# Weight magnitudes, float64 exponents and the leaky activation on ScalarE, c21 read from PSUM, and turn steps on either of two engines

## The chip, the core and the metric

The kernel runs on one core of one Trainium2 chip. The core has a matrix engine (PE; its weight loads are listed as PEld), a vector engine (DVE), a scalar engine (ACT), a general engine (POOL) and a sync engine (SP) that issues the DMAs. Each engine works through its own instructions strictly in program order; a semaphore holds an instruction, and all behind it, until what it needs is done. The metric is the device time of one execution in microseconds.

## The reference

Three layers follow one another. All arithmetic is float32, apart from the last layer's weights, which arrive as float64.

```python
# retention: B=4, H=8, S=576, D=64
scores = scale * np.matmul(q, k.transpose(0, 1, 3, 2))
ret = scores * Dmat[None, :, :, :]
x = np.matmul(ret, v)                 # -> (2304, 512)
# mixture: 8 experts, F=1024
P = np.exp(logits - logits.max())     # logits = x @ w_gate
for _ in range(8):
    P /= P.sum(1, keepdims=True) + 1e-09
    P /= P.sum(0, keepdims=True) + 1e-09
    P *= N / E
out += P[:, e:e + 1] * (np.maximum(x @ w1[e], 0.0) @ w2[e])
# feed-forward: d_ff=2048, float64 weights
h = x @ w_in
g = np.maximum(0.01 * h, h)
return g @ w_out
```

## The kernel before

**Units and stages.** The retention fills about the first 106 us. After it the two other layers are cut into 20 units of 512 hidden columns: units 0 to 15 are the mixture (two units per expert), units 16 to 19 the feed-forward layer. A unit runs through three stages of 384 token pairs, a stage through two groups g. Every group has seven *h products* (`product_h`, matmuls of line L916: inputs times first weights), and every stage 3 x 7 *second products* (`group_s`, L1089: hidden values times second weights). These are Strassen-like schemes with seven products in place of eight, so operands are sums and differences of quarter blocks. Units 0 and 15 (`PLAIN`) use an ordinary second product (L1131). Each float32 operand is split into a high and a low float16 part, and three of the four partial products are taken.

**Between the products.** ACT and DVE empty the banks. In a group the h products come in the order 1, 5, 6, 2, 7, 3, 4. Products 1, 6, 7 and 4 build on one another through ACT copies from bank to bank: hA to hB (L926), hB to hD (L943). c11, c12 and c22 end up in `fp`, c21 (from bank hD, L961) in the fourth quarter of `fs`, a buffer of which there is one. `splits` then queues the high parts (ACT, L999), the low parts (DVE, L1009 and L1006) and the sums and differences that the second products need (d1 L988, d2 L1037, d3 L1039, d4 L988 or L990). d1 and d3 read c21. In the feed-forward layer each block is first made leaky on DVE (L982). The second products are added into `y` by DVE (L1102); an ACT copy (L1107) seeds one bank from another.

**Weights.** While a unit runs, the next unit's weights are prepared (`prep_steps`): eight reductions on DVE find the largest magnitude of 512 columns each (`amax`, L167), L173 folds them, a matmul with ones (L179) adds the maxima of all partitions into every partition, and DVE turns the sum into a power of two (`pow2`, `recip2`). ACT scales the raw weights (L195), ACT makes the high parts (L210, L239), POOL the low parts and the block sums (L220, L227, L245). `idle_bank` lends such small matmuls the one of the two banks s1a and s1b that the pair of second products under way does not use; the next pair starts in that bank.

**Float64.** In units 0 to 14 the float64 weights come in 64 pieces: DVE masks mantissa and exponent (L343, L344), shifts the exponent's bias and clamps it (`first2`, L350 and L351), ACT makes the mantissa (L358), DVE joins the parts (L367, L368), POOL multiplies (L375).

**The turn.** Behind unit 15 (`turn_steps`) each block of `y` is normed by the sum of its magnitudes (ACT, L1207), scaled on POOL (L1223), transposed on PE, copied from the bank by ACT (L1235), and cut into operands: POOL sums, high parts on ACT (L477), low parts on DVE (L480), a store to DRAM and a load back (`x<-x`) for units 16 to 19.

**What sets the order.** No loop on the chip: the program is straight, and its order is worked out while it is written. PE's order is fixed in the main (`seconds_by`). `Order` keeps a clock of its own and a booked end for each engine (`COST`); at every tick it takes from its queues the tasks whose inputs are done by its booking and whose engine is free within 0.6 us (`SLACK`). `flush` forces what must stand before a product. `lat` is the extra time that a task is to stand behind its inputs.

## Time and profile before

| | us |
|---|---|
| median of three runs | 1950.81 (1947.8 to 1951.41) |
| the profiled execution | 1949.6 |
| its span, first to last instruction | 1947.8 |
| busy: PE / DVE / ACT / POOL | 1802.0 / 1697.6 / 1135.9 / 839.2 |
| mean granted clock of PE | 0.977 of full |

The span and the execution's own time lie 1.8 us apart. Stretches are given in us from the span's start; u3 is unit 3. In a row of the trace, busy time is the union of the instructions' times, while the mean is of one instruction: PE's matmuls overlap, so a mean of 330 ns does not mean that each costs 330 ns. "Idle before" is the time that the engine stood still just before such instructions, and the releaser is what ended it.

### The profile page before, as it was taken

To read this page: it belongs to the slowest core of one execution; us is meant where nothing else is said; L and a number is where in the kernel's file an instruction comes from. 1 tells how busy PE (TensorE), PEld (TensorE's weight loads), DVE (VectorE), ACT (ScalarE), POOL (GpSimd) and SP (SyncE) were. 2 spreads that over 40 slices of the span, in tenths; PEclk is the share of its full clock that TensorE was granted. 3 is DMA by queue.
4 is the path that set the end of the run, shared out by engine and by line. 5 is a ranking of instruction groups with operands and counts; after the bars stand their busy time and mean duration, and the time that the engine had idled before them with its cause. 6 is when DMAs were issued, how large, how long until landed. Compare 5 with 4: busy or idle time off the path is not lost.

```text
span 1947.8 us, 35674 instructions
## 1 busy us (share of the span) xinstructions
PE 1802.0 (93%) x13699; PEld 1298.0 (67%) x13699; DVE 1697.6 (87%) x2877; ACT 1135.9 (58%) x2294; POOL 839.2 (43%) x786
## 2 busy tenths in 40 slices
PE   8879999899999989999999999999999967899997
PEld 7744477677677767776776777677775545566776
DVE  6756799999999999999999999999866757699986
ACT  5645656465656656565665656465556557556542
POOL 4725353443627253452536254352428625273400
PEclk8889999999999999999999999999999989899999
DMA  8863353444454453444444354345343532343242
GB/s 309 300 215 116 127 179 115 144 130 141 133 163 123 127 180 107 147 136 155 125 151 146 111 179 130 123 133 179 97 126 109 191 122 78 119 139 97 76 126 76
DMA packets 207855, 276.64 MB, mean 142 GB/s; under 512 B 13874, under 2 KB 177860, under 8 KB 202564
## 3 DMA queue, kind: packets, MB, share of 16 engines
q1 hardware_dynamic: 207684, 274.37, 44.8%
q8 instruction: 107, 1.75, 0.4%
q14 instruction: 64, 0.52, 0.1%
HBM read 244.69 MB, written 29.63 MB: 141 GB/s over the span
## 4 chain that ended last, share of the span: by engine, by line
DVE 47%; PE 39%; issue 4%; POOL 4%; DMA 3%; ACT 2%; SPq 0%; DVEq 0%; ACTq 0%; POOLq 0%
DVE y L1102 10%; PE s L1089 6%; DVE hs L1009 6%; PE hB L916 5%; PE hA L916 5%; PE s1a L1089 5%; PE hE L916 5%; PE s1b L1089 4%; DVE fs L988 4%; DVE hp L1006 3%; DVE hp L1009 3%; PE hD L916 2%; DVE fs L1039 2%; DVE fs L1037 2%; PE s L1131 2%
## 5 line engine op out<-in xcount | busy, mean ns | idle before, releaser
L916 PEld LDWEIGHTS <-w 128*128 128x128 f16 x5040 | 495.5, 99 | 304.2 <-issue 34.8
L1089 PEld LDWEIGHTS <-hs 128*128 128x128 f16 x3888 | 381.3, 98 | 118.8 <-DVE hs L1009 19.2
L1089 PEld LDWEIGHTS <-hp 128*128 128x128 f16 x2916 | 287.0, 98 | 126.6 <-issue 50.4
L220 POOL TENSOR_TENSOR w<-raw,w 128x384 f16<-128x384 f32 x152 | 173.3, 1156 | 354.2 <-ACT w L210 354.2
L227 POOL TENSOR_TENSOR raw<-raw 128x256 f32<-128x256 f32 x304 | 289.6, 953 | 19.6
L916 PE MATMUL hE<-x,w 128*128 128x384 f16 x1440 | 278.4, 330 | 16.1 <-DMA x<-x 7.4
L916 PE MATMUL hB<-x,w 128*128 128x384 f16 x1440 | 276.6, 328 | 11.8 <-ACT hB L926 9.3
L916 PE MATMUL hA<-x,w 128*128 128x384 f16 x1440 | 278.8, 330 | 8.5 <-POOL w L220 7.1
L1089 PE MATMUL s<-w,hs 128*128 128x256 f16 x1944 | 266.3, 273 | 6.8 <-ACT s L1107 6.4
L999 ACT ACTIVATE hs<-fs 128x768 f16<-128x768 f32 (+1 forms) x228 | 188.0, 825 | 136.3 <-DVE fs L988 72.2
L245 POOL TENSOR_TENSOR w<-raw,w 128x512 f16<-128x512 f32 x148 | 201.4, 1376 | 119.1 <-ACT w L239 119.0
L1009 DVE TENSOR_TENSOR hs<-fs,hs 128x768 f16<-128x768 f32 (+1 forms) x228 | 238.1, 1057 | 5.5 <-ACT hs L999 5.4
L1102 DVE SCALAR_TENSOR_TENSOR y<-s,fac,y 128x256 f32<-128x256 f32 (+1 forms) x324 | 196.5, 608 | 52.3 <-PE s L1089 34.9
L375 POOL TENSOR_TENSOR f<-f,e 128x256 f32<-128x256 f32 x64 | 52.1, 813 | 394.7 <-DVE e L368 393.1
L999 ACT ACTIVATE hp<-fp 128x384 f16<-128x384 f32 x240 | 158.2, 678 | 39.9 <-DVE fp L954 27.6
L1089 PE MATMUL s1a<-w,hp 128*128 128x256 f16 x972 | 135.9, 277 | 28.6 <-DVE y L1102 28.6
L1089 PE MATMUL s1b<-w,hs 128*128 128x256 f16 x972 | 135.5, 273 | 13.6 <-DVE hs L1009 8.2
L1089 PE MATMUL s1a<-w,hs 128*128 128x256 f16 x972 | 137.6, 278 | 10.2 <-DVE hs L1009 5.9
L1089 PE MATMUL s1b<-w,hp 128*128 128x256 f16 x972 | 132.7, 273 | 12.1 <-DVE y L1102 11.9
L961 ACT ACTIVATE fs<-hD 128x384 f32<-128x384 f32 x120 | 58.8, 490 | 143.4 <-DVE hs L1009 96.7
L916 PE MATMUL hD<-x,w 128*128 128x384 f16 x720 | 137.9, 328 | 1.0 <-ACT hD L943 0.4
L1089 PE MATMUL s<-w,hp 128*128 128x256 f16 x972 | 133.9, 274 | 0.4 <-ACT s L1107 0.4
(175 smaller groups left out, 2773.1 us busy)
## 6 DMA issues: line engine op xcount, KB each, us to landing
x<-x SPq DMA_DIRECT2D x420, 384.0 KB, 4.1
raw<-in_wm SPq DMA_DIRECT2D x32, 1024.0 KB, 6.2
r<-in_wf SPq DMA_DIRECT2D x64, 256.0 KB, 3.3
qk<-in_qk SPq DMA_DIRECT2D x16, 512.0 KB, 6.8
vk<-in_vk SPq DMA_DIRECT2D x16, 512.0 KB, 4.8
wf_s<-f SPq DMA_DIRECT2D x32, 256.0 KB, 3.6
raw<-wf_s SPq DMA_DIRECT2D x8, 1024.0 KB, 5.2
x<-xst SPq DMA_DIRECT2D x30, 256.0 KB, 2.0
```

The lines of the kernel that those rows point to most:

```text
L220: nc.gpsimd.tensor_tensor(v[0], v[1], v[2], op=ALU.subtract)
L227: nc.gpsimd.tensor_tensor(o, x, y_, op=ALU.subtract)
L245: (nc.gpsimd if u or part else nc.vector).tensor_tensor(lo, r, hi, op=ALU.subtract)
L375: nc.gpsimd.tensor_tensor(dst, dst, cur["tx"].bitcast(F32), op=ALU.mult)
L916: nc.tensor.matmul(bank, w[:, a, wi, k, :], x[:, :, b, k, :], start=r in (1, 5) and k == q == 0, stop=k == 1 and q == 2, skip_group_check= ...
L961: nc.scalar.activation(tmp["fs"][:, 2], D_, AF.Relu if moe else AF.Copy, scale=HS)
L988: nc.vector.scalar_tensor_tensor(out_, a, 0.0, b, op0=ALU.max, op1=op)
L999: nc.scalar.activation(hid[k][:, 0, a:b], src[:, a:b], AF.Relu if moe and relu else AF.Copy)
L1006: nc.vector.scalar_tensor_tensor(t[:, 1, a:b], src[:, a:b], 0.0, t[:, 0, a:b], op0=ALU.max, op1=ALU.subtract)
L1009: nc.vector.tensor_tensor(t[:, 1, a:b], src[:, a:b], t[:, 0, a:b], op=ALU.subtract)
L1089: nc.tensor.matmul(out_, t[:, a, i, ts], w[:, b, wi, 0, :], start=start and k == 0, stop=k == 5, skip_group_check=True)
L1102: nc.vector.scalar_tensor_tensor(out_, bank, f, out_, op0=ALU.mult, op1=ALU.add)
```

## The change

Nothing is computed that was not computed before, apart from the scale that weights get. Five edits:

1. For units 1 to 19 `mags` takes the place of `amax`: ACT sums the magnitudes of 512 columns (an Abs activation with an accumulator output, its elements written to `junk`). Since a sum of magnitudes per partition takes the place of a largest one, `top` is longer: DVE adds the four partial sums of each half, PE turns the column into a row by two matmuls with the identity, DVE takes the row's largest value (`mr`), and a matmul with a row of ones hands it to all partitions. These matmuls use the idle bank. The fixed powers of two are set anew (`WS`, `HS`, `GW`).
2. `first2` goes; the exponent is masked in place and one Relu on ACT (`power`) shifts, scales and clamps it.
3. The leaky activation is one ACT function (Prelu with slope 0.01): for c11 and c21 it is the very step that empties the bank, c12 and c22 get a step of their own on ACT.
4. In units 1 to 14 c21 stays in bank hD: ACT applies Relu in place, and d1 and d3 read the bank. Before product 7 of the next group is copied into hD, the waiting tasks up to d3 are written out.
5. In the turn a task may be for "A" or "D": `emit` gives it to the engine that its booking says is free first. So it goes with the sums of magnitudes, the copies from the bank, and the high parts. The step that inverts the last third of `inv` leaves its fixed place in `drain` and becomes a task that waits 7 us behind the issue of its DMA.

```diff
-XS, W1S, W2S, HS = 2.0 ** 12, 2.0 ** 11, 2.0 ** 11, 2.0 ** -13
-YS = 1.0 / (XS * W1S * W2S * HS)
+XS, HS, GW = 2.0 ** 12, 2.0 ** -15, 2.0 ** 11
+WS = lambda u: 2.0 ** 13 if u else 2.0 ** 11
...
     def emit(self, x):
         after = max([d.done + LAT for d in x.deps], default=0.0)
+        if x.eng and len(x.eng) > 1:
+            e = min(x.eng, key=lambda e: (self.free[e] > self.t, self.free[e]))
+            x.done = self.book(e, x.n, after)
+            x.f(nc_of[e])
+            return
...
+        def mags(part, c):
+            def f():
+                nc.scalar.activation(junk, raws[u, part][:, 512 * c:512 * c + 512], AF.Abs,
+                                     accum_out=st["mx"][:, part, c:c + 1])
+            return f
+
         def top(p):
             def f():
-                nc.vector.reduce_max(st["m"][:, p], st["mx"][:, p], axis=AX.X)
+                if u == 0:
+                    nc.vector.reduce_max(st["m"][:, p], st["mx"][:, p], axis=AX.X)
+                    return
+                nc.vector.reduce_sum(st["m"], st["mx"], axis=AX.X)
+                bk = small_bank(f"wt{u}")
+                for part in range(2):
+                    nc.tensor.matmul(bk[:1, P * part:P * part + P], st["m"][:, part:part + 1], ident,
+                                     start=part == 0, stop=True, skip_group_check=True)
+                st["r"] = small.tile([1, 2], F32, tag="mrw", name=f"mr{u}", bufs=1)
+                nc.vector.reduce_max(st["r"], bk[:1, :2 * P].rearrange("p (a i) -> p a i", a=2), axis=AX.X)
             return f
...
-                nc.tensor.matmul(bk, ones_b, st["m"][:, p], start=True, stop=True)
+                if u:
+                    nc.tensor.matmul(bk, ones[:1, :], st["r"], start=True, stop=True)
+                else:
+                    nc.tensor.matmul(bk, ones_b, st["m"][:, p], start=True, stop=True)
...
-            return [add("D", 512, amax(part, c), (first_,), key, there) for c in range(4)]
+            return [add("A" if u else "D", 512, (mags if u else amax)(part, c), (first_,), key, there) for c in range(4)]
...
-            t_ = add("D", 40, top(p), mx_, key)
+            t_ = add("D", 40 if u == 0 else 400, top(p), mx_, key)
...
-                nc.vector.tensor_scalar(tx, hw, 20, 0x7FF, op0=ALU.logical_shift_right, op1=ALU.bitwise_and)
-            return f
-
-        def first2(n):
-            def f():
-                tx = cur["tx"]
-                nc.vector.tensor_scalar(tx, tx, -896.0, 0.0, op0=ALU.add, op1=ALU.max)
-                nc.vector.tensor_scalar(tx, tx, 255.0, 2.0 ** 23, op0=ALU.min, op1=ALU.mult)
+                nc.vector.tensor_scalar(tx, hw, 0x7FF00000, None, op0=ALU.bitwise_and)
...
+        def power(n):
+            def f():
+                nc.scalar.activation(cur["tx"], cur["tx"], AF.Relu, scale=8.0, bias=low_e)
+            return f
...
-            c = Task("D", 300, first2(n), (a,), "f64")
+            c = Task("A", 256, power(n), (a,), "f64")
...
-            h = add("A", 256 * n, high, dep, cond=room)
+            h = add("AD", 256 * n, high, dep, cond=room)
...
             load_inverse(2)
+            there = Task(None, 0, None, done=order.t + 7)
+            order.queues["gate"].append(Task("D", 20, lambda: recip2(inv_of(2), inv_of(2)), (there,), "inv"))
...
-                 (1, lambda: None), (1, lambda: None), (1, lambda: None), (1, lambda: recip2(inv_of(2), inv_of(2)))]
+                 ]
...
+    def bent(out_, in_, u, scale=1.0):
+        if u < NU1:
+            nc.scalar.activation(out_, in_, AF.Relu, scale=scale)
+        else:
+            nc.scalar.activation(out_, in_, AF.Prelu, scale=scale, alpha=SLOPE)
...
         elif r == 7:
+            order.flush("hid", lambda k: len(k) > 3 and k[:3] != (u, s, g))
             nc.scalar.copy(D_, B_)
...
-            order.flush("hid", lambda k: k != (u, s, g))
+            order.flush("hid", lambda k: k[:3] != (u, s, g))
             tmp["fs"] = work("fs", 4)
-            nc.scalar.activation(tmp["fs"][:, 2], D_, AF.Relu if moe else AF.Copy, scale=HS)
+            bent(tmp["fs"][:, 2] if u in PLAIN or u >= NU1 else D_, D_, u, HS)
...
-                d = add("D", ST, leaky(fp[:, 0]), (d,))
...
-                d = (add("D", 2 * ST, leaky(fp[:, 1:3]), d),)
+                d = (add("A", 2 * ST, lambda: bent(fp[:, 1:3], fp[:, 1:3], u), d),)
...
-                d = add("D", ST, leaky(fs[:, 2]), (d,))
-            d1 = add("D", ST, plus(fs[:, 0], a22, fs[:, 2], ALU.add), (d,) + tmp["a2"])
+            d1 = add("D", ST, plus(fs[:, 0], a22, a21, ALU.add), (d,) + tmp["a2"], None, moe)
...
-            d3 = add("D", ST, lambda: nc.vector.tensor_tensor(fs[:, 2], a11, fs[:, 2], op=ALU.subtract), (d1, d2))
+            d3 = add("D", ST, lambda: nc.vector.tensor_tensor(fs[:, 2], a11, a21, op=ALU.subtract), (d1, d2), None,
+                     moe)
...
-        a = add("A", 1224, sums(j), (y_done,))
-        a = add("D", 300, norms(j), (a,))
+        a = [add("AD", 512, sums(j, h), (y_done,)) for h in range(2)]
+        a = add("D", 300, norms(j), a)
...
-        t = [add("A", 512, turned(j, h), (b[h],) + p.get(f"x{h}", ()), 0.5) for h in range(2)]
+        t = [add("AD", 512, turned(j, h), (b[h],) + p.get(f"x{h}", ()), 0.5) for h in range(2)]
```

Three places show where instructions stand. The first is DVE in unit 7, as unit 8's weights get their scale. Before (`raw` are the raw weights, `mx` the partial results, `m` their fold, `pww` the first step of `pow2`):

```order
L1102 SCALAR_TENSOR_TENSOR y_1441<-s_0_1459,fac_7928,y_1441 128x256
L167 TENSOR_REDUCE mx_8505<-raw_1_8256 128x1
L1009 TENSOR_TENSOR hp_0_0_8651<-fp_8568,hp_0_0_8651 128x384
L173 TENSOR_REDUCE m_8503<-mx_8505 128x2
L1006 SCALAR_TENSOR_TENSOR hp_0_0_8651<-fp_8568,hp_0_0_8651 128x768
L1102 SCALAR_TENSOR_TENSOR y_1441<-s1a,fac_7928,y_1441 128x512
L988 SCALAR_TENSOR_TENSOR fs_8638<-fp_8568,fs_8638 128x384
L131 TENSOR_SCALAR pww_0_8714<-s1b 128x2
```

And now:

```order
L989 SCALAR_TENSOR_TENSOR fp_8568<-hB,p_42_8523 128x384 [waits Activation_49]
L994 SCALAR_TENSOR_TENSOR fp_8568<-hE,u_42_8550 128x384 [waits PE_49]
L197 TENSOR_REDUCE m_8495<-mx_8497 128x2 [waits Activation_49]
L203 TENSOR_REDUCE mr_8621<-s1a 1x2 [waits PE_49]
L144 TENSOR_SCALAR pww_0_8642<-s1b 128x2 [waits PE_49]
```

The reductions of `raw` are gone from DVE; the fold waits for ACT, and the row's largest value stands right behind the fold, waiting for PE. On PE the same place reads, before:

```order
L1089 MATMUL s_0_1459<-w_6_1_6965,hs_2_1_8547 128x256
L179 LDWEIGHTS ones_b
L179 MATMUL s1b<-m_8503,ones_b 128x2 [waits DVE_49]
L916 LDWEIGHTS w_7_1_8316
L916 MATMUL hA<-x_0_1_8385,w_7_1_8316 128x384
```

And now:

```order
L1125 LDWEIGHTS hs_1_1_8214
L1125 MATMUL s_1_1462<-w_6_1_6964,hs_1_1_8214 128x256
L200 MATMUL s1a<-ident,m_8495 1x128 [waits DVE_49]
L200 MATMUL s1a<-ident,m_8495 1x128
L1125 LDWEIGHTS hp_2_0_8335
L1125 MATMUL s1a<-w_6_0_6943,hp_2_0_8335 128x256 [waits DVE_49]
```

The two matmuls with the identity write the bank s1a that the next pair of second products takes at once. So it is in the odd units from 3 to 13; in most of the others an h product stands between the two. The second place is ACT, a little ahead of the first, where bank hB is copied into hD. Before:

```order
L938 ACTIVATE fp_8568<-hA 128x384
L999 ACTIVATE hs_2_1_8547<-fs_8478 128x768
L943 COPY hD<-hB 128x384
L1107 COPY s_1_1460<-s_1_1460 128x256
L1107 COPY s_0_1459<-s1a 128x256
```

And now:

```order
L943 ACTIVATE fp_8568<-hA 128x384
L188 ACTIVATE junk,mx_8497<-raw_0_8463 128x512 x2
L983 COPY hD<-hB 128x384
L188 ACTIVATE junk,mx_8497<-raw_0_8463 128x512 x2
L188 ACTIVATE junk,mx_8497<-raw_1_8239 128x512
L1143 COPY s_1_1462<-s_1_1462 128x256
```

Five of the eight sums of magnitudes stand around the copy into hD. The third place is ACT in unit 16, where unit 17's first weights (`w_17_0`) are cast; groups are counted through the program from 0, and unit 16 has the groups 96 to 101. Before, the first cast stands in group 100:

```order
L1099 ACTIVATE y_1437<-s1a,fac_18210 128x256
L195 ACTIVATE raw_0_17827<-raw_0_17827,sw_0_18136 128x512
L1107 COPY s_0_1459<-s_0_1459 128x256
L999 ACTIVATE hs_1_1_18549<-fs_18399 128x768 x2
L210 CAST w_17_0_18562<-raw_0_17827 128x3x128 x2
```

Now it stands in group 98 (the number in p_98 is the group's):

```order
L965 COPY hB<-hA 128x384
L228 ACTIVATE raw_0_17753<-raw_0_17753,sw_0_17983 128x512
L969 ACTIVATE p_98_18115<-hE 128x384
L243 CAST w_17_0_18128<-raw_0_17753 128x3x128
L973 ACTIVATE u_98_18134<-hB 128x384
L243 CAST w_17_0_18128<-raw_0_17753 128x3x128
```

What moved is the preparation of unit 17's weights, by two groups. In the turn, 13 of the 40 high parts, 12 of the 18 copies from a bank and 8 of the 18 sums of magnitudes now stand on DVE.

## Rows read from the trace of the kernel before

**Rows 1.** Stretches: length; busy us (instructions) of PE, PEld, DVE, ACT, POOL; clock; DMA.

```profile
106.10:189.20 83.10, 72.10 (x512) 39.77 (x511) 47.86 (x118) 47.35 (x92) 31.84 (x36) 0.95 0.53 172
189.20:285.40 96.20, 91.83 (x581) 57.07 (x580) 82.85 (x164) 58.50 (x111) 48.59 (x46) 0.98 0.45 139
285.40:378.70 93.30, 85.92 (x634) 62.67 (x632) 88.85 (x153) 52.78 (x105) 39.47 (x38) 0.96 0.46 141
378.70:1333.40 954.70, 917.65 (x6943) 679.60 (x6941) 919.54 (x1532) 575.42 (x1149) 429.27 (x401) 0.99 0.45 140
...
1333.40:1519.70 186.30, 179.17 (x1243) 121.07 (x1241) 143.49 (x248) 113.91 (x232) 83.68 (x79) 1.00 0.41 128
1519.70:1632.90 113.20, 90.23 (x564) 56.64 (x563) 80.54 (x139) 67.25 (x141) 46.02 (x39) 0.92 0.43 138
1632.90:1742.90 110.00, 89.09 (x633) 62.49 (x632) 85.91 (x124) 65.59 (x131) 65.03 (x57) 0.94 0.34 105
1742.90:1947.80 204.90, 188.00 (x1443) 140.95 (x1441) 173.18 (x275) 96.62 (x191) 36.80 (x33) 0.99 0.32 97
```

**Rows 2.** Timeline of PE, unit 12: start, length, what [idle before, releaser].

```profile
1155.02 1.14 PE L916 MATMUL hE<-x,w 128*128 128x384 f16 x6
1155.99 0.82 PE L1089 MATMUL s<-w,hs 128*128 128x256 f16 x6
1156.65 1.14 PE L916 MATMUL hD<-x,w 128*128 128x384 f16 x6
...
1227.11 1.44 PE L1089 MATMUL s1a<-w,hp 128*128 128x256 f16 x6 [2.52 <-DVE y L1102]
```

**Rows 3.** Waits of PE, units 3 to 13: us, times, longest.

```profile
PE s1a L1089 <- DVE y L1102: 19.3, 10, 2.5
PE s1b L1089 <- DVE y L1102: 7.0, 11, 0.8
PE s L1089 <- ACT s L1107: 6.0, 11, 0.8
```

**Rows 4.** Instructions of DVE: what, shapes, count, busy, mean ns, idle before.

```profile
L988 DVE SCALAR_TENSOR_TENSOR fs<-fp,fs 128x384 f32<-128x384 f32 x168 | 126.5, 753 | 4.1 <-ACT fs L961 4.1
...
L167 DVE TENSOR_REDUCE mx<-raw 128x1 f32<-128x512 f32 x160 | 104.6, 674 | 17.8 <-DMA raw<-wf_s 17.8
...
L949 DVE SCALAR_TENSOR_TENSOR fp<-hB,p 128x384 f32<-128x384 f32 x120 | 65.4, 545 | 5.1 <-ACT hD L943 4.8
...
L982 DVE SCALAR_TENSOR_TENSOR fp<-fp 128x384 f32<-128x384 f32 (+1 forms) x48 | 43.4, 909 | 1.7 <-ACT fp L938 1.7
...
L350 DVE TENSOR_SCALAR e<-e 128x256 int32<-128x256 int32 x64 | 36.0, 562 | 0.3
```

**Rows 5.** Instructions near to the new ones, same columns.

```profile
L358 ACT ACTIVATE f<-f 128x256 f32<-128x256 int32 x64 | 26.4, 412 | 23.1 <-DVE f L343 23.1
...
L1207 ACT ACTIVATE tab<-y 128x512 bf16<-128x512 f32 x18 | 11.3, 629 | 1.5 <-DVE y L1102 1.3
...
L1207 ACT ACTIVATION_READ_ACCUMULATOR tab<-y 128x1 f32 x18 | 3.4, 189 | 0.0
...
L847 PE MATMUL s1a<-ident,mx 128*1 128x128 f32 x2 | 0.4, 271 | 0.0
...
L848 DVE TENSOR_REDUCE mrow<-s1a 1x1 f32<-1x128 f32 x1 | 0.3, 278 | 1.9 <-PE s1a L847 1.9
```

**Rows 6.** Timeline of unit 0, DVE and PE.

```profile
120.64 0.17 DVE L137 TENSOR_SCALAR inv<-inv 128x6 int32<-128x6 int32 x1 [6.25 <-DMA inv<-s_dram]
...
122.32 1.12 PE L916 MATMUL hE<-x,w 128*128 128x384 f16 x3 [4.58 <-DVE fp L954]
```

**Rows 7.** Waits of PE, units 16 and 17.

```profile
PE hE L916 <- DMA x<-x: 7.4, 1, 7.4
PE hA L916 <- POOL w L220: 7.1, 1, 7.1
PE hB L916 <- ACT hB L926: 6.7, 2, 4.6
```

81 lines of the change are left out of this document (44 added, 37 removed).

## The prediction

> **What bounds the kernel now.** I read the busy times stretch by stretch first, then PE's timeline in one unit, then who makes PE wait. Over units 3 to 13 PE is busy 96% of 954.7 us and DVE 96% as well, ACT 60%, POOL 45% [rows 1]. Both cannot be the bound, so the timeline has to say which is. Where nothing holds PE, an h product of six matmuls follows the next instruction at 0.97 us and a second product of six at 0.66 us (differences of the starts) [rows 2]. A unit has 42 h products and 63 second products: 42 x 0.975 + 63 x 0.656 = 82.3 us. Eleven such units would be 905 us, and they take 954.7: some 49 us above the floor. Of these, 26 us are waits for DVE's additions to `y`, which come late because DVE is behind; 6 us are waits for ACT [rows 3]. One such wait of 2.52 us stands directly before products that run at about half pace (six matmuls in 1.44 us, where 0.82 is usual) [rows 2], and the stretch's granted clock is 0.99 [rows 1], between 5 and 14 us of 954.7 by its rounding; I take 5. So PE sets the pace, and DVE, full to 96%, adds the waits on top. Elsewhere DVE is not full: at the turn (1519.7 to 1742.9) PE is busy 90.2 and 89.1 us of 113.2 and 110.0, at a clock of 0.92 and 0.94 [rows 1], and it waits for loads, for POOL's weights and for ACT [rows 7].
>
> **What leaves DVE.** The reductions: 152 of the 160 go, at 0.674 us each, 102 us [rows 4]. The two exponent steps: 128 x 0.56 = 72 us [rows 4]. The leaky steps: 43 us, and 24 more on c21 that at half of the 909 ns mean bound above are 11 us, 54 us in all, all behind 1519.7 [rows 4]. c21 from the bank: d1 took 753 ns reading two SBUF operands, whereas L949, the same operation with one operand in a bank, took 545 [rows 4]. 84 instructions of d1 gain about 0.2 us each; for 84 of d3, which has no row here, I take from nothing to 0.2 us. Together 17 to 34 us, and I take 28. On the other side the turn gives DVE 33 short operations (some 20 us at 0.5 to 0.7) and `top` 19 reductions of at least 0.278 us [rows 5], 5 us. DVE loses about 230 us. In units 3 to 13 alone it is 88 reductions (59 us), about two thirds of the exponent steps (50 us) and of c21 (20 us): from 919.5 to about 790 us, 85 to 87% of what would then be left.
>
> **What comes to ACT.** 152 sums. The row of the same form has 629 ns plus 189 for reading the accumulator [rows 5], 0.82 us: 124 us. 64 exponent steps at 0.412 us [rows 5] or a little more, 26 to 33 us. 24 leaky steps on 768 columns, which no row here shows; between half and all of a microsecond, 12 to 24 us. The turn gives back some 20. ACT rises by about 150 us, over units 3 to 13 from 60% to some 72%. This lies beside PE's work as long as ACT's evacuations stay in time. In the first groups of a unit they are not free of it: five of the eight sums stand around the copy into hD, and what is queued behind them is the seeding copy and the next evacuation of c21.
>
> **The added waits.** PE now waits at the two matmuls with the identity for DVE's fold, and the fold for ACT's last sum. Between the end of the hB product that the copy into hD needs and the matmuls with the identity, PE has 12 second-product matmuls, an h product and six more: 1.3 + 0.97 + 0.66 = 2.9 us. In this time ACT must copy (about 0.5 us) and make three sums (3 x 0.82), then DVE folds: 3.2 to 3.5 us. So PE stands for 0.3 to 0.6 us. In the odd units the next second products use the same bank: on PE they are queued behind two matmuls of at least 0.27 us and DVE's 0.278 us [rows 5], with a passage between engines each way, about 1 us more. From below the price is nothing (ACT ahead), from above it is that of the longest wait shown, 2.52 us [rows 2]. I take 1.3 us in an odd unit and 0.7 in another. On DVE the first step of `pow2` then waits for PE, with additions to `y` behind it; DVE's idle 13% covers that. ACT's copy into hD now waits for d3 of the group before; d3 stands about eight DVE instructions ahead, and in return ACT no longer waits for `fs` to come free before it takes c21. I cost this pair at nothing.
>
> **The sum by stretches [rows 1].** To 106.1 nothing moves that PE waits for.
> - Unit 0: DVE stands 6.25 us for the DMA of `inv`, and PE 4.58 us for the DVE work behind it [rows 6]. The step moves behind five operand instructions and the logits. I take the 4.6 us and 1.4 of the 4 us that a clock of 0.95 cost: -6.
> - Unit 1: 4.4 us not busy, clock 0.98: -2.
> - Unit 2: 7.4 us not busy, clock 0.96: 11 us above what PE needs, three quarters go: -8.
> - Units 3 to 13: of the 49 us above the floor, DVE's waits fall from 26 and a few to 3, the clock's 5 go, ACT's 6 become 9, and the exchange adds 6 x 1.3 + 5 x 0.7 = 11. That leaves 49 - 23 - 5 + 3 + 11 = 35 and, as a part of DVE's small waits goes too, I take 31: -18.
> - Units 14 and 15: 7 us not busy: -3.
> - Unit 16: 23 us not busy and 9 us of clock. The last high parts of the turn stand about a group earlier on ACT, or on DVE; of the waits for loads and ACT (7.4 and 6.7) [rows 7] about 6 go, and 3 of the clock: -9.
> - Unit 17: 21 us not busy and 6 us of clock. Its weights start two groups earlier, so most of the wait for POOL (7.1) [rows 7] goes and some of the rest: 8, and 3 of the clock: -11.
> - Units 18 and 19: 17 us not busy; DVE loses the leaky steps: -5.
>
> Together -62 us. The profiled execution took 1949.6 us, its span 1947.8; 1949.6 - 62 = 1888, and the median of the runs, 1950.8, lies 1.2 above it: **1888 us** after rounding.
>
> **Rivals.**
> *ACT becomes the late engine (0.20).* In the first two or three groups of a unit it has eight sums (6.6 us) and the prescales beside its evacuations. If evacuations slip behind sums, PE's waits only change their name: the 18 us of units 3 to 13 and the 8 of unit 2 are lost, and at the turn half of the 20. 1888 + 26 + 10 = 1924. For it: the planner books less for a sum than 0.82 us; in order, a late sum delays every evacuation behind it. Against it: ACT made PE wait only 6 us in 954.7 [rows 3], and 28% of it stay free. The Trainium skill, "ScalarE: Activation LUTs", section "Rules for kernel authors", speaks for this rival: simple operations such as relu, max and add belong on VectorE. The rows agree with it per instruction (0.82 us against 0.67 [rows 4, 5]); whether it decides hangs on which engine is late.
> *Nearly all waits go (0.12).* If the exchange hides behind PE's queue and the turn's order runs as booked, units 2 to 13 end 8 + 18 + 20 lower instead of 26, and the turn 35 instead of 20: 1888 - 20 - 15 = 1853.
> *The exchange through the idle bank costs more than DVE gave (0.05).* The place is the matmul with the identity, 19 times. If ACT is so late that PE stands 2.5 us and then runs at half pace as behind the wait in unit 12, a time costs some 4 us: 19 x 4 = 76 against the 73 of gain without the exchange, about 1953 to 1960. It decides from about 3.8 us each. Against it: only one of two banks is touched, and the wait comes once a unit.
> *Nothing to be seen (0.04).* DVE's waits give way to as much elsewhere, within 0.2% of 1950.8, which is about what a measurement of this kernel can tell from no change.
> *The turn's choice does nothing.* Excluded as to the order: 33 operations did go to DVE. If they wait there for stores as they did on ACT, this costs the 9 us of unit 16, which is inside the range.
>
> **How the numbers follow.** The forecast has 0.59, with 1870 to 1908 as its own spread. Faster: 0.59 + 0.20 + 0.12 = 0.91; same 0.04; slower 0.05. The range reaches from the lower rival to past the ACT rival: 1850 to 1935.
>
> **What would show it.** Right: DVE busy for about 1465 us, ACT for some 1285; units 3 to 13 in about 937 us with hardly any wait of PE for `y`; PE's waits before the matmuls with the identity 0.3 to 1 us; unit 17 without a wait of 7 us for POOL; the clock above 0.985. The first step to fall would be the size of the added waits: if PE stands more than 2 us at each, or waits for ACT more than 20 us in units 3 to 13, the ACT rival holds. The second is the turn, where an order that differs in many places decides, and two thirds of the 20 us could as well not come.

## The result and the profile after the change

The changed kernel takes 1871.7 us (median of four runs, 1870.9 to 1872.7) against 1951.1 us for the kernel before in the same comparison: a ratio of 0.959, with a 95% interval of 0.958 to 0.961. The prediction was right in direction and range (1850 to 1935); its value, 1888 us, was 16 us too high. The profiled execution took 1871.1 us, its span 1869.4. What lies ahead of unit 0 varies by itself: 104.1 to 112.0 us over the runs below, whatever the edit, so the 1.9 us there need not come from the change.

The table sets the predicted differences beside the measured ones; the measured ones are stretches of the changed kernel (below) less those of [rows 1].

| stretch | before | after | measured | predicted |
|---|---|---|---|---|
| ahead of unit 0 | 106.1 | 104.2 | -1.9 | 0 |
| unit 0 | 83.1 | 79.4 | -3.7 | -6 |
| unit 1 | 96.2 | 95.7 | -0.5 | -2 |
| unit 2 | 93.3 | 86.3 | -7.0 | -8 |
| units 3 to 13 | 954.7 | 921.6 | -33.1 | -18 |
| units 14 and 15 | 186.3 | 190.0 | +3.7 | -3 |
| unit 16 | 113.2 | 106.1 | -7.1 | -9 |
| unit 17 | 110.0 | 88.6 | -21.4 | -11 |
| units 18 and 19 | 204.9 | 197.5 | -7.4 | -5 |
| together | 1947.8 | 1869.4 | -78.4 | -62 |

The rows answer to [rows 1] and have its columns: the stretch, its length, busy time of PE, PEld, DVE, ACT and POOL, then the granted clock.

```profile
0.00:104.20 104.20, 86.35 (x1163) 75.93 (x1164) 75.03 (x136) 58.58 (x144) 57.53 (x62) 0.89 0.86 302
104.20:183.60 79.40, 72.10 (x518) 39.82 (x517) 42.70 (x104) 51.94 (x107) 30.13 (x34) 0.97 0.53 175
183.60:279.30 95.70, 92.40 (x587) 57.25 (x587) 70.14 (x138) 65.29 (x132) 47.16 (x45) 0.98 0.44 132
279.30:365.60 86.30, 83.77 (x638) 61.97 (x636) 76.76 (x135) 58.68 (x124) 38.48 (x39) 1.00 0.50 150
365.60:1287.20 921.60, 916.83 (x6998) 682.70 (x6997) 802.60 (x1384) 660.51 (x1386) 418.88 (x406) 1.00 0.48 147
1287.20:1477.20 190.00, 182.84 (x1252) 122.54 (x1251) 132.41 (x227) 117.02 (x246) 80.96 (x76) 0.99 0.40 126
1477.20:1583.30 106.10, 92.16 (x570) 57.44 (x569) 81.31 (x136) 67.24 (x140) 55.37 (x51) 0.94 0.43 138
1583.30:1671.90 88.60, 85.83 (x638) 62.28 (x636) 63.88 (x98) 70.55 (x146) 36.45 (x32) 0.98 0.39 118
1671.90:1869.40 197.50, 186.53 (x1448) 141.04 (x1446) 141.89 (x228) 112.31 (x223) 49.77 (x45) 0.99 0.35 106
```

In units 3 to 13 PE is now busy 916.8 of 921.6 us, at a clock of 1.00; DVE has come down from 96% to 87%, ACT has risen from 60% to 72%. What PE still waits for there is all of it new (compare [rows 3]): the fold of the partial sums (L197) and the row's largest value (L203).

```profile
PE s1a L1125 <- DVE mr L203: 3.0, 6, 0.5
PE s1a L200 <- DVE m L197: 1.8, 6, 0.7
```

The waits for `y` (26 us) are gone, and so are those for ACT (6 us). What ACT itself waited for in these units shows why. In the kernel before, what held it longest were DVE's results and the buffer `fs`, which DVE empties:

```profile
ACT hs L999 <- DVE fs L988: 63.1, 50, 2.8
ACT fs L961 <- DVE hs L1009: 62.4, 27, 6.0
```

In the changed kernel it waits for PE:

```profile
ACT s L1143 <- PE s L1125: 55.2, 64, 2.5
ACT hD L943 <- PE hD L955: 36.7, 45, 1.8
```

The new and shortened operations, grouped by line with shapes kept apart (mean ns of one stands after the busy time; compare [rows 4, 5]):

```profile
L188 ACT ACTIVATE junk<-raw 128x512 bf16<-128x512 f32 x152 | 95.2, 626 | 1.7 <-DMA raw<-wf_s 0.3
L188 ACT ACTIVATION_READ_ACCUMULATOR junk<-raw 128x1 f32 x152 | 28.9, 190 | 0.0
L391 ACT ACTIVATE e<-e,low_e 128x256 int32<-128x256 int32 x64 | 31.8, 498 | 0.0
L945 ACT ACTIVATE fp<-fp 128x768 f32<-128x768 f32 x24 | 20.2, 840 | 5.9 <-DVE fp L994 5.9
L1025 DVE SCALAR_TENSOR_TENSOR fs<-fp,fs 128x384 f32<-128x384 f32 x84 | 62.5, 744 | 0.0
L1025 DVE SCALAR_TENSOR_TENSOR fs<-fp,hD 128x384 f32<-128x384 f32 x84 | 45.7, 544 | 1.2 <-ACT hD L943 0.9
L1073 DVE TENSOR_TENSOR fs<-fp,hD 128x384 f32<-128x384 f32 x84 | 45.5, 542 | 0.0
```

A sum on ACT costs 0.626 + 0.190 = 0.816 us, as taken; the exponent step 0.498 (taken: 0.412 or a little more), the leaky step on 768 columns 0.840 (taken: 0.5 to 1). c21 in the bank saves 0.2 us in d1 (L1025), and in d3 (L1073) 0.146 against the 688 ns of d3 (L1039) in the kernel before, inside its bounds. Both savings are of means; the last section shows what the means are made of. DVE is busy 1486.7 us in all (predicted 1465), ACT 1262.1 (predicted 1285).

And this is PE's own sequence in an even unit (unit 8): the exchange. Columns: start, length, line, operation; there is no wait in it.

```profile
796.77 0.82 PE L1125 MATMUL s1b<-w,hs 128*128 128x256 f16 x6
797.56 0.60 PE L200 MATMUL s1a<-ident,m 128*1 128x128 f32 x4
798.09 1.15 PE L955 MATMUL hD<-x,w 128*128 128x384 f16 x6
799.07 0.82 PE L1125 MATMUL s<-w,hp 128*128 128x256 f16 x6
799.73 0.65 PE L955 MATMUL hA<-x,w 128*128 128x384 f16 x3
800.31 0.38 PE L210 MATMUL s1a<-mr,ones 1*128 1x2 f32 x2
800.62 0.66 PE L955 MATMUL hA<-x,w 128*128 128x384 f16 x3
801.12 0.82 PE L1125 MATMUL s<-w,hs 128*128 128x256 f16 x6
```

The trace lists the two matmuls with the identity as four instructions. From the start of the second product at 796.77 to that of the next product are 1.32 us where 0.66 is usual, and the interrupted h product takes 1.39 us where 0.97 is usual: 0.66 + 0.42 = 1.08 us of PE's own time, without a wait. In an odd unit (unit 7) the same place holds two waits as well, since the next second products use the bank:

```profile
711.36 0.82 PE L1125 MATMUL s<-w,hs 128*128 128x256 f16 x6
712.39 0.60 PE L200 MATMUL s1a<-ident,m 128*1 128x128 f32 x4 [0.21 <-DVE m L197]
713.49 0.81 PE L1125 MATMUL s1a<-w,hp 128*128 128x256 f16 x6 [0.50 <-DVE mr L203]
```

Here 2.13 us lie between two second products that are 0.66 apart otherwise: 1.47, and with the 0.42 of the row of ones 1.89 us.

### The profile page after: what moved, and what is told of

Read it like the earlier page. It is cut to its first block, busy times and chain, and to the rows that moved or that the text cites. A ratio compares the mean times of both kernels' runs of the same rounds, so it can differ in the third digit from the quotient of the medians.

```text
span 1869.4 us, 35931 instructions
## 1 busy us (share of the span) xinstructions
PE 1798.8 (96%) x13794; PEld 1301.0 (70%) x13794; DVE 1486.7 (80%) x2578; ACT 1262.1 (68%) x2645; POOL 814.7 (44%) x786
## 4 chain that ended last, share of the span: by engine, by line
PE 81%; DVE 9%; POOL 4%; ACT 3%; DMA 2%; issue 2%; SPq 0%; DVEq 0%; ACTq 0%; POOLq 0%
PE s L1125 15%; PE hB L955 11%; PE hA L955 11%; PE s1a L1125 11%; PE hE L955 11%; PE s1b L1125 10%; PE hD L955 5%; DVE y L1138 2%; PE s L1167 2%; POOL raw L260 1%; DVE hs L1046 1%; PE s1b L1167 1%; PE s1a L1167 1%; DMA s_dram<-s 1%; POOL y L1261 1%
## 5 line engine op out<-in xcount | busy, mean ns | idle before, releaser
L253 POOL TENSOR_TENSOR w<-raw,w 128x384 f16<-128x384 f32 x152 | 164.5, 1096 | 331.2 <-ACT w L243 306.2
L260 POOL TENSOR_TENSOR raw<-raw 128x256 f32<-128x256 f32 x304 | 285.1, 938 | 20.2
L1046 DVE TENSOR_TENSOR hs<-fs,hs 128x768 f16<-128x768 f32 (+1 forms) x228 | 244.1, 1086 | 11.8 <-ACT hs L1036 11.6
L278 POOL TENSOR_TENSOR w<-raw,w 128x512 f16<-128x512 f32 x148 | 191.3, 1308 | 92.7 <-ACT w L272 92.4
L1138 DVE SCALAR_TENSOR_TENSOR y<-s1b,fac,y 128x512 f32<-128x512 f32 (+1 forms) x163 | 99.7, 612 | 51.1 <-ACT s L1143 22.3
L1138 DVE SCALAR_TENSOR_TENSOR y<-s1a,fac,y 128x256 f32<-128x256 f32 (+1 forms) x161 | 98.3, 611 | 47.0 <-ACT s L1143 28.9
```

The lines of the kernel that those rows point to most:

```text
L253: nc.gpsimd.tensor_tensor(v[0], v[1], v[2], op=ALU.subtract)
L260: nc.gpsimd.tensor_tensor(o, x, y_, op=ALU.subtract)
L278: (nc.gpsimd if u or part else nc.vector).tensor_tensor(lo, r, hi, op=ALU.subtract)
L1046: nc.vector.tensor_tensor(t[:, 1, a:b], src[:, a:b], t[:, 0, a:b], op=ALU.subtract)
L1138: nc.vector.scalar_tensor_tensor(out_, bank, f, out_, op0=ALU.mult, op1=ALU.add)
```

## The experiments

Theory: PE sets the pace, DVE was late because it was full, and ACT was late because it waited for DVE; so the change gains about what DVE's lateness cost, less what the exchange costs. Rivals: ACT becomes the late engine; the gain hangs on the exchange's place; the gain came from another order of the work. All kernels below are the changed kernel with the edit shown, unless said otherwise. Ratios are to the kernel before, with 95% intervals; busy shares and lengths come from each run's profile.

| run | us | ratio | units 3 to 13 | DVE, ACT busy there | units 16 + 17 |
|---|---|---|---|---|---|
| before | 1951.1 | 1 | 954.7 | 96%, 60% | 223.2 |
| after | 1871.7 | 0.959 (0.958 to 0.961) | 921.6 | 87%, 72% | 194.7 |
| sums_dve | 1909.0 | 0.979 (0.977 to 0.982) | 926.5 | 91%, 65% | 220.3 |
| dve_load | 1920.0 | 0.985 (0.982 to 0.988) | 953.2 | 89%, 69% | 198.3 |
| act_double | 1984.3 | 1.017 (1.014 to 1.021) | 989.2 | 81%, 73% | 204.5 |
| edit1_alone | 1925.5 | 0.988 (0.986 to 0.991) | 931.0 | 93%, 68% | 221.9 |
| turn_act | 1906.6 | 0.978 (0.976 to 0.980) | 922.2 | 87%, 72% | 231.0 |
| f64_dve | 1880.2 | 0.965 (0.962 to 0.967) | 920.9 | 89%, 69% | 194.2 |
| c21_sbuf | 1875.7 | 0.963 (0.960 to 0.967) | 924.1 | 90%, 71% | 194.6 |
| one_matmul | 1850.1 | 0.949 (0.947 to 0.952) | 904.9 | 88%, 73% | 196.8 |
| no_edit1 | 1874.7 | 0.962 (0.960 to 0.964) | 906.8 | 92%, 66% | 215.3 |
| one_matmul_act_double | 1916.1 | 0.983 (0.981 to 0.984) | 943.0 | 84%, 76% | 204.1 |
| leaky_dve | 1875.2 | 0.962 (0.960 to 0.963) | 921.6 | 87%, 72% | 195.3 |
| sums_act_late | 1855.7 | 0.952 (0.951 to 0.954) | 906.8 | 92%, 66% | 195.0 |

### sums_dve: the sums back on DVE

```diff
-                nc.scalar.activation(junk, raws[u, part][:, 512 * c:512 * c + 512], AF.Abs,
-                                     accum_out=st["mx"][:, part, c:c + 1])
+                nc.vector.tensor_reduce(st["mx"][:, part, c:c + 1], raws[u, part][:, 512 * c:512 * c + 512],
+                                        axis=AX.X, op=ALU.add, apply_absolute_value=True)
```

> The sums of the weights' magnitudes go back to DVE (152 reductions of about 0.67 us, 102 us), the exchange through the idle bank and the four other edits stay. If DVE was late because it was full, as the prediction has it, DVE returns in units 3 to 13 from 87% to about 94%, waits of PE for the additions to y come back in the even units (1 to 3 us each, and the clock of such a unit falls below 1.00), and the time is 1884 to 1897 us. If the other edits alone have freed enough of DVE, or if the gain of units 2 to 13 came from another order of the work, it stays within 4 us of the changed kernel, 1868 to 1876 us. ACT loses some 120 us of work; if ACT had been the late engine, the time would fall below 1866 us.

Measured: 1909.0 us, more than either theory had. But the loss isn't where the load theory put it: units 3 to 13 take only 4.9 us more, with DVE at 91%; unit 17 takes 114.1 us in place of 88.6. There a reduction of the next unit's raw weights stands at the head of DVE for 23.1 us until their load lands. But PE's longest wait is for this unit's own weights, and the load, on SP, could only start when POOL was done with them (the last line is of units 16 and 17 together):

```profile
DVE mx L188 <- DMA raw<-wf_s: 23.1, 1, 23.1
PE hA L955 <- ACT w L243: 9.0, 1, 9.0
PE hE L955 <- ACT w L272: 2.0, 1, 2.0
SPq L167 <- POOL w L278: 46.7, 4, 32.7
```

So the sums on ACT mattered less as load than by when unit 17's weights are ready; DVE's long wait comes from the same lateness (more under unit 17 below). In the middle units the load theory is only bounded here: with the four other edits DVE at 91% is early enough.

### dve_load: only the load put back

```diff
             def f():
+                nc.vector.tensor_reduce(st["un"][:, part, c:c + 1], raws[u, part][:, 512 * c:512 * c + 512],
+                                        axis=AX.X, op=ALU.max, apply_absolute_value=True)
                 nc.scalar.activation(junk, raws[u, part][:, 512 * c:512 * c + 512], AF.Abs,
```

> The changed kernel with 152 idle reductions added on DVE, one beside each of ACT's sums, each as long as the one that the change took away (its result goes nowhere). Only DVE's load is put back; ACT's work and every other position stays. If DVE's load is the cause, the time rises as with the sums back on DVE, by 12 to 25 us to 1884 to 1897, with PE's waits for y back in the even units. If what mattered was where the sums and the folding stand, or the other edits, it stays within 4 us of the changed kernel.

Measured: 1920.0 us; units 3 to 13 lose 31.6 us. The forecast of a rise held, its mechanism did not: PE hardly waits for `y`. It waits for the fold:

```profile
PE s1a L203 <- DVE m L200: 23.4, 11, 4.3
PE s1b L1128 <- DVE y L1141: 0.3, 1, 0.3
```

Several of the idle reductions stand on DVE just ahead of the fold, for which PE waits at the matmuls with the identity. So this run doesn't separate load from order, as it was meant to. It shows that the exchange's place has no room: what delays the fold delays PE.

### act_double: each sum made twice

```diff
-                nc.scalar.activation(junk, raws[u, part][:, 512 * c:512 * c + 512], AF.Abs,
-                                     accum_out=st["mx"][:, part, c:c + 1])
+                for _ in range(2):
+                    nc.scalar.activation(junk, raws[u, part][:, 512 * c:512 * c + 512], AF.Abs,
+                                         accum_out=st["mx"][:, part, c:c + 1])
```

> Each of ACT's 152 sums is made twice, 0.82 us more each, 124 us in all; ACT in units 3 to 13 goes from about 72% to some 85%. The prediction's main case (ACT has room, PE hardly waits for it) expects 1872 to 1882 us, the additional time at the exchange: up to 1 us in a unit, since the fold waits for ACT's last sum. The rival in which ACT is the late engine expects PE's waits for ACT and for the fold to rise by more than 1.5 us a unit and the time above 1895 us.

Measured: 1984.3 us, slower than the kernel before, so the forecast that ACT has room for this fell. Units 3 to 13 lose 67.6 us while ACT is busy 718.5 of 989.2 us, 73%. It isn't full; one chain through it is late:

```profile
PE s1a L201 <- DVE m L198: 44.6, 11, 4.9
PE s1a L1126 <- DVE mr L204: 3.0, 6, 0.5
```

Nearly all of PE's waits are for the fold (44.6 us, 1.8 in the changed kernel); for two of ACT's own copies it waits 0.3 us each. The other 24 us of the 67.6 are PE's own work taking longer (940.5 us busy, 916.8 in the changed kernel) at a granted clock of 0.97. Unit 5, for one, was at 1.00 in the changed kernel (84.1 us):

```profile
567.60:658.30 90.70, 85.69 (x639) 63.01 (x637) 71.71 (x125) 64.69 (x142) 36.91 (x36) 0.96 0.44 135
```

This is the prediction's third rival, the exchange dearer than the gain: real as a mechanism, and held off by less than one more round of sums (8 x 0.816 = 6.5 us of ACT's work in a unit). In unit 5 PE stands 4.5 us for the fold instead of 0.2.

### edit1_alone: the kernel before with the first edit

```diff
-            return [add("D", 512, amax(part, c), (first_,), key, there) for c in range(4)]
+            return [add("A" if u else "D", 512, (mags if u else amax)(part, c), (first_,), key, there) for c in range(4)]
...
-                nc.tensor.matmul(bk, ones_b, st["m"][:, p], start=True, stop=True)
+                if u:
+                    nc.tensor.matmul(bk, ones[:1, :], st["r"], start=True, stop=True)
+                else:
+                    nc.tensor.matmul(bk, ones_b, st["m"][:, p], start=True, stop=True)
```

(with the fold, the matmuls with the identity and the scales of the first edit.)

> The kernel before with the first edit alone: the sums on ACT and the exchange through the idle bank. DVE loses about 97 us, in units 3 to 13 from 96% to some 90%. If DVE's load is the cause in units 2 to 13, most of PE's waits for y go and these units lose 20 to 35 us, while the turn keeps its 113 and 110 us: 1916 to 1931 us. If DVE stays late at 90%, or if the other edits brought the gain, less than 10 us are seen: 1941 us or more.

Measured: 1925.5 us, inside the load theory's bounds. Units 3 to 13 take 931.0 us: with DVE at 93% the first edit alone brings 23.7 of their 33.1 us. Units 16 and 17 gain next to nothing (221.9 against 223.2 us); in unit 17 PE still stands for its weights, although no engine waits there for the load of the next ones longer than 0.8 us:

```profile
PE hA L955 <- ACT w L243: 6.6, 1, 6.6
```

Unit 0 keeps PE's wait of 4.6 us for `fp` [rows 6], which belongs to the fifth edit.

### turn_act: no choice of engine in the turn

```diff
-            h = add("AD", 256 * n, high, dep, cond=room)
+            h = add("A", 256 * n, lambda: high(nc.scalar), dep, cond=room)
```

(and so for the sums and the copies.)

> The turn's sums, copies and high parts are written for ACT alone, as before; the four other edits stay. Theory A: the choice of engine brought most of what the turn gained (units 16 and 17: 223.2 us before, 194.7 in the changed kernel); then unit 17 goes back to 105 to 112 us with PE's waits for weights in it, and the time is 1888 to 1899 us. Theory B: the choice does nothing by itself, and unit 17 gained from the other edits, whose lighter DVE lets the turn's work come out in another order; then unit 17 stays below 92 us and the time at 1868 to 1877 us. Units 2 to 13 stay as they are in both.

Measured: 1906.6 us. Theory A holds and is too small: units 16 and 17 take 231.0 us, 36.3 more than in the changed kernel, and 7.8 more than before the change. In unit 17 PE waits for ACT's casts of its weights, and over both units DVE waits for the high parts on ACT (2.4 us in the changed kernel):

```profile
PE hA L955 <- ACT w L243: 14.5, 2, 11.8
DVE hp L1046 <- ACT hp L1036: 27.4, 8, 15.4
```

and in unit 17 the load of the next raw weights, on SP, waits for POOL up to 40.3 us, 10.1 in the changed kernel:

```profile
SPq L167 <- POOL w L278: 47.8, 2, 40.3
```

With the sums added to it and no help in the turn, ACT is late.

### f64_dve: the exponents back on DVE

```diff
-                nc.scalar.activation(cur["tx"], cur["tx"], AF.Relu, scale=8.0, bias=low_e)
+                tx = cur["tx"]
+                nc.vector.tensor_scalar(tx, tx, -896.0, 0.0, op0=ALU.add, op1=ALU.max)
+                nc.vector.tensor_scalar(tx, tx, 255.0, 2.0 ** 23, op0=ALU.min, op1=ALU.mult)
```

> The exponent's shift and clamp go back to DVE (two steps of 0.56 us, 64 times, 72 us; ACT loses some 32 us). DVE in units 3 to 13 rises from 87% to about 92%. With the sums back on DVE these units took 926 us at 92% against 921.6 in the changed kernel, so, if only the load counts, they take 923 to 929 us and the whole 1873 to 1880 us. If the prediction's proportional reckoning holds (50 us of DVE of the 129 that it loses there, with 33 us gained), it is 12 us: 1883 us or more. If an emptier ACT helps the exchange, the time falls below 1869 us.

Measured: 1880.2 us, 0.5% above the changed kernel by the ratios. Units 3 to 13 do not lose (920.9 us). Units 5, 7, 9 and 11 take 83.8 instead of 84.1, since there the exchange now uses the bank that the next pair does not need: the fold costs PE 0.4 us instead of 0.2, but the 0.5 us for the row's largest value are gone. Unit 2 loses 3.1 us, with DVE busy 81.8 of its 89.4 us. So the proportional reckoning fell: beyond what the first edit gave, more room on DVE brings nothing in the middle units.

### c21_sbuf: c21 copied to SBUF

```diff
-            bent(tmp["fs"][:, 2] if u in PLAIN or u >= NU1 else D_, D_, u, HS)
+            bent(tmp["fs"][:, 2], D_, u, HS)
...
-            a21 = hD[:, :ST] if moe else fs[:, 2]
+            a21 = fs[:, 2]
```

> c21 is copied to SBUF again in units 1 to 14, and d1 and d3 read it there (0.2 to 0.24 us more each, 84 times each, some 34 us of DVE); ACT waits again for the buffer fs to come free. DVE in units 3 to 13 rises from 87% to 90%. If only DVE's load counts: units 3 to 13 0 to 3 us longer, 1872 to 1877 us. If ACT's waiting for fs held back the sums that stand behind it and so the fold that PE waits for: 0.5 us or more in each unit, 1880 to 1890 us.

Measured: 1875.7 us. Units 3 to 13 take 924.1 us, 2.5 more, unit 2 2.4 more. The load theory holds, and ACT's wait for `fs` costs PE nothing once DVE is early.

### one_matmul: the exchange as it was before

```diff
-                for part in range(2):
-                    nc.tensor.matmul(bk[:1, P * part:P * part + P], st["m"][:, part:part + 1], ident,
-                                     start=part == 0, stop=True, skip_group_check=True)
-                st["r"] = small.tile([1, 2], F32, tag="mrw", name=f"mr{u}", bufs=1)
-                nc.vector.reduce_max(st["r"], bk[:1, :2 * P].rearrange("p (a i) -> p a i", a=2), axis=AX.X)
...
-                if u:
-                    nc.tensor.matmul(bk, ones[:1, :], st["r"], start=True, stop=True)
-                else:
-                    nc.tensor.matmul(bk, ones_b, st["m"][:, p], start=True, stop=True)
+                nc.tensor.matmul(bk, ones_b, st["m"][:, p], start=True, stop=True)
```

> The sums stay on ACT, but the exchange between the partitions is the one of the kernel before: one matmul with a matrix of ones adds the partitions' sums (in bf16), in place of two matmuls with the identity, DVE's largest value of the row and a matmul with a row of ones; the fixed power of two is set to 2^20 for it. If the exchange costs what PE's row shows (0.7 us of waits in an odd unit, none in an even one) and two matmuls of 0.27 us besides, units 3 to 13 lose 0.5 us each and the odd ones 1.2: 1858 to 1868 us in all. If PE is at its floor for other reasons and waits for the fold all the same, it stays within 3 us of the changed kernel: 1869 to 1875 us.

Measured: 1850.1 us, faster than both kernels and below the range that I gave. Units 3 to 13, and two units one after the other (7 and 8):

```profile
362.90:1267.80 904.90, 904.83 (x6944) 678.33 (x6942) 792.62 (x1365) 659.49 (x1381) 419.63 (x405) 1.00 0.49 149
```

```profile
692.10:774.30 82.20, 82.20 (x633) 61.63 (x631) 70.70 (x124) 59.44 (x126) 37.07 (x36) 1.00 0.49 148
774.30:856.60 82.30, 82.30 (x634) 61.71 (x633) 73.11 (x126) 60.87 (x129) 39.31 (x38) 1.00 0.49 154
```

A unit takes 82.2 to 82.3 us, which is the floor that the prediction worked out from the products (82.3), and PE is busy all of it. In the changed kernel an even unit is 1.08 and an odd one 1.9 us longer; 5 x 1.08 + 6 x 1.89 = 16.7 us, and 921.6 - 904.9 = 16.7. The exchange is all that the changed kernel still pays there.

### no_edit1: the four other edits

Beside the edit of one_matmul, the maxima on DVE and the power of two of the kernel before:

```diff
-            return [add("A" if u else "D", 512, (mags if u else amax)(part, c), (first_,), key, there) for c in range(4)]
+            return [add("D", 512, amax(part, c), (first_,), key, there) for c in range(4)]
```

> The four other edits without the first: DVE's reductions of the largest magnitudes and the one matmul with ones, as before the change, and no exchange through the identity. With the exchange as one matmul the units 3 to 13 took 904.9 us, at PE's floor; with the sums on DVE beside the long exchange 926.5 us at 90% of DVE. If DVE at some 92% is early enough, they take 905 to 912 us here, and the first edit as it stands has cost more than it brought in these units. Whether the whole is better hangs on unit 17: if it falls back to 114 us, as with the sums on DVE, the time is 1876 to 1890 us; if it stays near 88 us, 1850 to 1862 us. If DVE is late again at 92% and more, units 3 to 13 take over 920 us.

Measured: 1874.7 us. Units 3 to 13 take 906.8 us with DVE at 92%: without the first edit they are 14.8 us shorter than with it. But unit 17 takes 111.5 us; PE stands there again for its weights, and DVE for the load of the next ones:

```profile
PE hA L942 <- ACT w L230: 8.9, 1, 8.9
DVE mx L181 <- DMA raw<-wf_s: 22.3, 1, 22.3
```

### one_matmul_act_double: ACT's room without the exchange

The edits of one_matmul and act_double together.

> The kernel with one matmul for the exchange, and each of ACT's sums made twice as in the run that doubled them (124 us more on ACT). If the 113 us that the doubling cost there came from the place of the exchange (PE stands at its first matmul directly behind the fold, and the fold behind ACT's last sum), the later place of the single matmul takes most of it away: 1855 to 1885 us, and PE's waits for ACT's evacuations stay under 1 us a unit. If ACT with more work is late at everything, the time is above 1930 us, with waits for evacuations and seeding copies.

Measured: 1916.1 us, 66 above one_matmul, between the two forecasts. Of PE's waits in units 3 to 13 most are still for the fold, nearly all of them in the odd units (19.1 us; 1.5 in the even ones):

```profile
PE s1b L204 <- DVE m L198: 19.1, 6, 3.2
PE s L1117 <- ACT s L1135: 4.2, 5, 0.9
PE s1a L204 <- DVE m L198: 1.5, 5, 0.3
```

The later place of the single matmul takes 29.5 of the 67.6 us away that the doubling cost in these units (943.0 - 904.9 = 38.1), not most of it. ACT's seeding copies begin to make PE wait (0.9 us in an even unit): ACT's room is between one and two times the sums.

### leaky_dve: the leaky steps back on DVE

```diff
-            nc.scalar.activation(out_, in_, AF.Prelu, scale=scale, alpha=SLOPE)
+            nc.scalar.activation(out_, in_, AF.Copy, scale=scale)
...
-                d = (add("A", 2 * ST, lambda: bent(fp[:, 1:3], fp[:, 1:3], u), d),)
+                d = (add("D", 2 * ST, leaky(fp[:, 1:3]), d),)
```

(and a step on DVE for c11 and for c21.)

> The leaky activation is made again in steps of its own on DVE (some 54 us, all behind unit 15; ACT loses its 24 steps of 768 columns, some 20 us). The prediction had -5 us for units 18 and 19 from this edit. If DVE's load is what counts, unit 18 goes back towards its 90.4 us with PE's waits for the low parts on DVE, and unit 17 rises by a few us: 1878 to 1888 us. If the turn's order flips as it did with the sums on DVE, unit 17 takes over 105 us: 1892 us or more. If DVE has room enough there, it stays within 3 us of the changed kernel.

Measured: 1875.2 us, 0.2% above the changed kernel. Unit 18 takes 86.1 us instead of 84.3, and unit 19 1.1 more; the turn keeps its order (195.3 us). It lies between the first and the last case; the edit would be worth some 4 us, but the intervals of the two kernels overlap.

### sums_act_late: on ACT from unit 16 on

```diff
-            return [add("A" if u else "D", 512, (mags if u else amax)(part, c), (first_,), key, there) for c in range(4)]
+            return [add("A" if u >= 16 else "D", 512, (mags if u >= 16 else amax)(part, c), (first_,), key, there) for c in range(4)]
```

(with the edit of one_matmul.)

> Only the weights of units 16 to 19 have their magnitudes summed on ACT; those of units 1 to 15 keep DVE's largest magnitudes, and both use the one matmul with ones. In the runs with the reductions on DVE, DVE stood 22 to 23 us at one of them in unit 17 for the load of raw weights, and unit 17 took 111.5 and 114.1 us. If that wait at the head of DVE is what costs unit 17 its gain, it falls to 85 to 93 us here, units 2 to 13 stay as in the run without the first edit (about 990 us for both together), and the time is 1848 to 1858 us. If the turn's order hangs on something else that the sums change earlier, unit 17 stays above 105 us and the time at 1870 us or more.

Measured: 1855.7 us. Unit 17:

```profile
1566.20:1656.30 90.10, 84.60 (x633) 61.67 (x631) 62.00 (x101) 70.77 (x145) 33.29 (x32) 0.98 0.38 116
```

It falls from 111.5 to 90.1 us, and the only difference from no_edit1 is that the last four units' weights have their magnitudes summed on ACT instead of their largest taken on DVE. So the maxima on DVE in these last units are what cost it. That it was by DVE's wait for the load isn't shown: the fold of unit 17's weights, made in unit 16, moves as well. It stands 44.2 us after that unit's start (1457.90) in no_edit1, and 22.8 us after it (1461.30) here:

```profile
1502.11 0.15 DVE L193 TENSOR_REDUCE m<-mx 128x2 bf16<-128x8 f32 x1
```

```profile
1484.12 0.15 DVE L197 TENSOR_REDUCE m<-mx 128x2 bf16<-128x8 f32 x1
```

The eight reductions on DVE are spread over 35 us of unit 16, with the turn's own steps between them, the eight sums on ACT over 14. Whether this kernel or one_matmul is faster, the intervals (0.951 to 0.954, 0.947 to 0.952) don't settle.

## Why the prediction was right, and where its sizes were off

**What bounds the kernel.** Right. The floor of 82.3 us for a unit stands as measured in one_matmul. (A small slip: 790 us of DVE in the 937 forecast would be 84%, not 85 to 87; measured are 802.6 in 921.6.)

**Units 3 to 13 (-18, measured -33).** Two terms were off, and they partly cancelled. First, beside the exchange the sum let 20 of the 49 us above the floor stay (31 - 11): 3 of DVE's waits, ACT's waits risen from 6 to 9, and 8 of a rest of 12 without a name. None of it stayed. The failing step, for 9 of the 20, is to have taken ACT's waits for ACT's own. In the kernel before, ACT stood 63.1 and 62.4 us for DVE's results and for the buffer that DVE empties; its lateness was DVE's at second hand, and went with it. For 8 more it is to have let a rest without a name stay. PE was busy 917.7 us in the kernel before [rows 1], and 904.8 in one_matmul for as many matmuls: 12.8 us of longer work, of which the prediction booked 5 as clock. Where the other 8 lay isn't shown; they are gone with the waits.

The waits don't shrink in proportion to DVE's load either: 96% gave 954.7 us, 93% (edit1_alone) 931.0 with the exchange, 92% (no_edit1) 906.8 without it, 88% 904.9.

The other term is the exchange, 16.7 us measured for 11 taken. Its waits were smaller than priced (4.8 us in eleven units); the mis-sized part is PE's own work. The prediction counted it in the odd units alone, as two matmuls of 0.27 us, but its row (L847, x2) is one matmul, which the trace lists as two instructions. The two matmuls with the identity are four instructions, the one with the row of ones two more: 1.08 us each time, about as long as an h product, in every unit, where PE has nothing to spare.

What no run shows is that DVE's fullness by itself made the waits for `y`: none fills DVE to 96% again in the new order, and edit1_alone, on which this rests, changes the order too.

**Unit 17 (-11, measured -21).** The mechanism was right, its size was not. In the kernel before PE waited 11.2 us in this unit for its own weights (the 7.1 of [rows 7], and 4.1 more for POOL and ACT), in the changed one 2.3. The prediction took 8 us for this and some of the rest, and 3 for the clock; but of the 21 us not busy only 2.8 are left. What decides is how early the weights get their scale, that is, the fold in unit 16:

| run | fold, us after unit 16's start | PE's waits in unit 17 for its weights | DVE's wait for the next load | unit 17 |
|---|---|---|---|---|
| before | 41.1 | 11.2 | 17.8 | 110.0 |
| after | 22.8 | 2.3 | none | 88.6 |
| sums_dve | 44.2 | 12.8 | 23.1 | 114.1 |
| no_edit1 | 44.2 | 12.8 | 22.3 | 111.5 |
| edit1_alone | 44.3 | 12.6 | none | 110.1 |
| turn_act | 82.5 | 21.8 | none | 115.6 |
| dve_load | 25.7 | 2.3 | 2.5 | 88.0 |
| sums_act_late | 22.8 | 0 | none | 90.1 |

With the fold at 23 to 26 us the unit takes 88 to 90 us, with the fold at 41 or later 110 to 116, whether or not DVE waits for a load; the other six runs have it at 21 to 27 us and take 87 to 92. So a row of the kernel before that looks like the cause, over units 16 and 17, is second-hand:

```profile
DVE mx L167 <- DMA raw<-wf_s: 17.8, 1, 17.8
```

The load that it waits for stands on SP up to 24.0 us for POOL, which still works on this unit's raw weights. Both edits are needed for an early fold: with the first alone units 16 and 17 take 221.9 us, without it 215.3, without the choice of engine 231.0, with both 194.7. In the three slower runs the engine that makes the sums has much of the turn's work between them. So the rival that the turn's choice does nothing is false, by 36 us. No run moved the fold by itself; that it decides is read from these traces.

**Units 14 and 15 (-3, measured +3.7).** The wrong sign. Unit 14 takes 0.8 us less, unit 15 4.4 more (96.0): it has an exchange of its own (1.08 us), 0.9 us more of waiting for POOL's `y` (3.2 in all), 0.4 at the fold and 0.2 at a copy; the rest comes with a clock of 0.98, where it was 1.00. The prediction booked no exchange in these two units.

**Units 0, 1, 2, 16, 18 and 19.** Right within 2.5 us each.

**The rivals.** *ACT becomes the late engine*: not at this load (no wait of PE for ACT in units 3 to 13), but nearer than "28% of it stay free" suggests; with each sum doubled the kernel is slower than before although ACT is busy only 73%. What counts is the chain from the last sum through the fold to PE, not the share. The Trainium skill, "ScalarE: Activation LUTs", section "Rules for kernel authors", gives additions and maxima to VectorE. By the instruction the trace agrees (0.816 us on ACT, 0.674 on DVE [rows 4]). In the middle units the choice hardly tells (906.8 us with maxima on DVE and one matmul, 904.9 with sums on ACT); in the turn the runs go the other way (unit 17 takes 111.5 us with maxima on DVE, 90.1 with sums on ACT), since there the slower instruction on ACT comes to stand earlier. *Nearly all waits go*: this is what happened to the waits, though not to the exchange. *The exchange dearer than the gain*: not here, but act_double shows the mechanism.

**What each edit is worth beside the others**, by the ratios: the choice in the turn 1.9% (36 us), the exponents 0.5%, c21 0.4% with an interval that reaches nothing, the leaky step 0.2% and the first edit 0.2%, neither of them clear of the intervals. The first edit's gain in the turn is nearly paid back by its exchange. With the cheaper exchange it gains 1.0% more.

## What to carry to other kernels

When an engine is late, ask what each wait of the others waits for in turn before you book it as their own; take the late engine a little below full, and the waits that hang on it go together rather than one by one. A small operation on the engine that sets the pace costs its own time, even when nobody waits: count its instructions as the trace lists them. And where an engine stands long for a load, ask what held the load back: here DVE's 17.8 to 23.1 us were the far end of a chain that began some 20 us late at a small fold, one unit earlier.
